# A planner that counts VectorE's and GpSimd's shared port, keeps margins in VectorE's order, and clears the output later

## The chip, the cores and the metric

One core of one Trainium2 chip. The metric is the device time of the whole program in microseconds, the median of three runs. Engines are called PE (TensorE, products), DVE (VectorE), ACT (ScalarE), POOL (GpSimd) and SP (SyncE, which here issues the DMAs).

## What is computed

Three layers in a row: attention with random features, a dense layer of experts ("moe") and a layer that sends each token to one of eight experts ("moe2"). Inputs to `moe` are float64 in memory.

```python
def phi(x):                                   # q, k: 2 x 8 x 576 x 64, omega: 128 x 64
    proj = np.einsum('bhsd,md->bhsm', x, omega)
    h = proj - np.sum(x * x, axis=-1, keepdims=True) / 2.0
    return np.exp(h - np.max(h, axis=-1, keepdims=True)) / np.sqrt(m)
kv = np.einsum('bhsm,bhsd->bhmd', k_p, v); z = np.sum(k_p, axis=2)
x = num / den                                 # 1152 tokens x 512
...
h = x @ w_in                                  # 512 x 2048
g = h * np.clip(h + 3.0, 0.0, 6.0) / 6.0
x = g @ w_out                                 # 2048 x 512
...
expert_idx = np.argmax(x @ w_gate, axis=1)    # 8 experts, at most 288 tokens each
h = np.maximum(np.einsum('ecd,edf->ecf', disp, w1), 0.0)
y = np.einsum('ecf,efd->ecd', h, w2)
out[i] = gate_w[i] * y[expert_idx[i], pos[i]] # rows of tokens left out stay 0
```

## The kernel before

**Products in two halves.** Each float32 operand of the large products is kept as two float32r tiles, a high part (a copy on ScalarE) and a low part (operand minus high part, on VectorE or GpSimd), and a product is three matmuls.

**Attention** runs over 18 units (4 heads' worth of rows each, k and q mixed). A unit has a high part `XH` (ScalarE, L778), a low part `XL` (L780; units 2 to 17 on GpSimd), two halves of feature products `B` (PE, L790, into one of two `pj` buffers, for five units partly `tp`), the row maximum `N` of each half (VectorE, L796, `nm`), four exponentials `P` (ScalarE, L802, `phi`), for k the sums `K` (L817), for q a transposition `C`/`T` (L847, L851), the product with the sums `D` (L863, `nd`), the division `R`, `S`, `X` (VectorE, L873 to L885), a transposition `E` (L891) and the two halves of the token tile, `EH` (ScalarE) and `EL` (VectorE, L917).

**The first expert layer.** w_in and w_out are 16 blocks each, called i0 to i15 and o0 to o15, in groups of four (i0 to i3, o0 to o3, i4 to i7, ...). A block is loaded as int64 words into one of four `raw` buffers and unpacked by five passes `W0` to `W4` (L248, L250, L252, L254, L256) on VectorE; `W4` frees the `raw` buffer for the next load. For blocks from the thirteenth on (o4 and later), the first pass is an absolute value on ScalarE (L246). A block of w_in is then halved: `w` (ScalarE, L262) and `WL`, the low part (L264; before on GpSimd for i0 to i7, on VectorE for i8 to i15). The hidden product `H` of block f for token group g (three groups of 384 tokens) is 12 matmuls on PE (L277, tile `hp`, alternately in two `pj` and four `tp` buffers of PSUM), followed by `Ht` (ScalarE, L281), the gate product `Hg` (VectorE, L285, tile `g`) and a store `Hs` on SP (L287, for group 0 a second, L290). Of w_out each block is transposed on PE, `T` (L299, tile `tpW`, after its `W4`), copied by ScalarE (L302), and folded with the gate's weights once four are there (`G`, L309; `U`, L318), for the gate's logits `L` (L334). Three or four products `H` already stand between the last units of attention.

**After that** come the routing (small operations on VectorE), the products with w_out for 288 chosen tokens (L571), the expert's two layers (L639, L661, L689) for two windows, and indirect writes of the rows to `out`, which has been cleared before (`clear_out`: GpSimd blanks a tile, SP writes it to all of `out` by one DMA of 2304 KB).

**What sets the order.** `Plan` is a list scheduler that runs while the program is built. Each step has an engine, a cost in us, steps it comes after, buffers that it takes and frees, and a rank. `order` repeatedly takes, over all engines, the step that can begin first, and on one engine the lowest rank among those that can begin at once. The begin is the latest of: the engine's free time, `early`, and the end of what it comes after plus a hop. The steps are emitted in that order, so each engine's queue is the planner's; on the chip an engine works its queue in order and waits for data by semaphores alone. No time of the plan is enforced. For attention's steps `DELTA` adds a number to the rank by kind of step and by third of the units (0: units 0 to 4, 1: 5 to 12, 2: 13 to 17); the numbers come from a search over plans. SP's loads stand in the order of `LOADS`, each after a buffer has come free.

## Time and profile before

| what | value |
|---|---|
| runs shown | 331.89 us median (331.43 to 333.74) |
| the profiled execution | 332.73 us, its span 330.9 us |
| PE busy | 306.9 us (93%) |
| VectorE busy | 222.3 us (67%) |
| ScalarE busy | 177.5 us (54%) |
| GpSimd busy | 65.4 us (20%) |
| mean granted clock of TensorE | 0.990 |

How to read the rows below. A row of the windows has, for a stretch in us from the span's start, its length, the busy us of PE, PE's weight loads, VectorE, ScalarE and GpSimd, each with its number of instructions in brackets, then the granted clock (1.00 is full speed), the share of time that the DMA engines were busy, and GB/s. A row of the waits says which engine and line waited for which, then us in total, times, and the longest. A row in order of time has the start, us, the engine, line, operation, tiles, shapes and number, and in square brackets idle time just before it and what ended that. A row of the groups has the number of instructions, busy us and the mean in ns, and then idle time before them. The chain's rows have start, us and what. A row of the DMA issues has the number, KB each and the median us from issue to landing. `hp` is the hidden product, `tpW` the transposed w_out, `nm` the row maximum, `phi` the exponential, `x` and `wo` are blocks of w_in and w_out being unpacked.

### The profile page before, as it was taken

What the parts mean: (1) busy time and instruction counts of PE and PEld (TensorE: products, weight loads), DVE (VectorE), ACT (ScalarE), POOL (GpSimd) and SP (SyncE); (2) the same over time, 40 slices, a digit from 0 to 9 for tenths busy, and PEclk for the clock granted to TensorE, in tenths of its full rate; (3) what the DMA queues carried; (4) which work ended last, traced back from release to release, by engine and by line L of the source; (5) the groups of instructions that cost most, each with busy time, mean ns of one, the idle gap of its engine ahead of it and who ended that gap; (6) DMA issues with size and microseconds to landing.
All of it is one profiled execution on the core that took longest, in us unless ns stands there. A gap on an engine that the chain in (4) does not pass through costs nothing.

```text
span 330.9 us, 6974 instructions
## 1 busy us (share of the span) xinstructions
PE 306.9 (93%) x2570; PEld 278.7 (84%) x2570; DVE 222.3 (67%) x474; ACT 177.5 (54%) x427; POOL 65.4 (20%) x68
## 2 busy tenths in 40 slices
PE   8985989999997798999999999898999999999992
PEld 5884978999987596887989888698999989999781
DVE  5589899999999889889985354749955002764100
ACT  6988799984643545453766324533555132633110
POOL 0774813400240000000000000411513012511021
PEclk9998999999999999999999999999999999999998
DMA  7998662124458777877235127891770004710011
GB/s 245 362 317 309 248 231 66 64 90 137 138 176 254 263 226 234 271 229 223 97 127 184 49 74 244 280 318 57 235 255 1 2 24 101 274 50 0 4 48 32
DMA packets 29675, 54.10 MB, mean 163 GB/s; under 512 B 5536, under 2 KB 18208, under 8 KB 29632
## 3 DMA queue, kind: packets, MB, share of 16 engines
q1 hardware_dynamic: 29248, 52.38, 48.2%
q0 software_dynamic: 384, 1.18, 1.1%
q8 instruction: 22, 0.36, 0.5%
q14 instruction: 21, 0.17, 0.2%
HBM read 37.42 MB, written 16.13 MB: 162 GB/s over the span
## 4 chain that ended last, share of the span: by engine, by line
PE 51%; DVE 15%; DMA 15%; issue 9%; ACT 4%; POOL 2%; SPq 1%; POOLq 0%; ACTq 0%; DVEq 0%
PE hp L277 14%; PE yw L571 14%; PE hp L639 6%; DMA raw<-in_w_in_dram 4%; PE yq L661 4%; PE pj L790 4%; DMA raw<-in_w_out_dram 3%; PE nd L863 3%; DVE nm L796 2%; DMA rawe<-in_w_dram 2%; PE lg L334 2%; DMA out_dram<-scratch,to 2%; DVE g L285 2%; DMA rawx<-in_k_dram 2%; DVE x L252 2%
## 5 line engine op out<-in xcount | busy, mean ns | idle before, releaser
L277 PE MATMUL hp<-xT,wsplit 128*128 128x384 f32 x576 | 107.8, 340 | 0.0
L277 PEld LDWEIGHTS hp<-xT,wsplit 128*128 128x128 f32 x576 | 98.9, 188 | 5.1 <-issue 5.0
L618 POOL TENSOR_TENSOR wsplit<-rawe,wsplit 128x512 fp32r<-128x512 f32 x16 | 22.0, 1379 | 160.6 <-ACT wsplit L616 141.6
L571 PE MATMUL yw<-gh,ohi 128*128 128x288 f32 x256 | 51.9, 298 | 0.2 <-ACT scratch L701 0.2
L281 ACT ACTIVATE t<-hp,three 128x384 f32<-128x384 f32 x48 | 27.6, 578 | 31.4 <-PE hp L277 30.1
L802 ACT ACTIVATE phi<-pj,nm 128x128 f32<-128x128 f32 x144 | 41.0, 414 | 5.5 <-DVE nm L796 5.4
L571 PEld LDWEIGHTS yw<-gh,ohi 128*128 128x128 f32 x256 | 40.8, 188 | 1.3 <-issue 0.6
L285 DVE SCALAR_TENSOR_TENSOR g<-t,hp 128x384 f32<-128x384 f32 x48 | 26.4, 549 | 18.3 <-ACT t L281 17.5
L564 DVE TENSOR_TENSOR gh<-gw,gh 128x288 fp32r<-128x288 f32 x32 | 18.0, 578 | 30.1 <-ACT gh L562 27.8
L571 PE MATMUL yw<-gh,olo 128*128 128x288 f32 x128 | 37.6, 294 | 0.0
L790 PE MATMUL pj<-wbd,xh 128*128 128x256 f32 x144 | 26.3, 305 | 6.5 <-ACT phi L802 5.7
L796 DVE TENSOR_REDUCE nm<-pj 128x4 f32<-128x512 f32 x36 | 24.6, 684 | 5.5 <-ACT phi L802 3.6
L790 PEld LDWEIGHTS pj<-wbd,xh 128*128 128x128 f32 x144 | 19.7, 192 | 10.1 <-ACT phi L802 7.6
L780 POOL TENSOR_TENSOR xl<-rawx,xh 128x512 fp32r<-128x512 f32 x16 | 21.7, 1361 | 30.7 <-ACT xh L778 17.5
L562 ACT ACTIVATE gh<-gw 128x288 fp32r<-128x288 f32 x32 | 14.0, 442 | 23.7 <-PE yw L571 21.1
L639 PE MATMUL hp<-dT,wsplit 128*128 128x288 f32 x192 | 26.3, 296 | 0.4 <-DVE dT L583 0.4
L639 PEld LDWEIGHTS hp<-dT,wsplit 128*128 128x128 f32 x192 | 25.7, 188 | 0.6 <-DVE dT L583 0.6
L571 PEld LDWEIGHTS yw<-gh,olo 128*128 128x128 f32 x128 | 24.1, 189 | 0.0
L616 ACT ACTIVATE wsplit<-rawe 128x512 fp32r<-128x512 f32 x32 | 19.0, 622 | 1.3 <-DMA rawe<-in_w_dram 1.1
L264 POOL TENSOR_TENSOR wsplit<-x,wsplit 128x512 fp32r<-128x512 f32 x8 | 11.6, 1450 | 29.9 <-ACT wsplit L262 29.9
L689 PE MATMUL yp<-wsplit,h 128*96 128x512 f32 (+1 forms) x96 | 16.9, 337 | 0.0
L689 PEld LDWEIGHTS yp<-wsplit,h 128*96 128x96 f32 x96 | 13.5, 162 | 3.4
(147 smaller groups left out, 454.0 us busy)
## 6 DMA issues: line engine op xcount, KB each, us to landing
gall<-g SPq DMA_DIRECT2D x48, 192.0 KB, 3.1
raw<-in_w_in_dram SPq DMA_DIRECT2D x16, 512.0 KB, 4.8
raw<-in_w_out_dram SPq DMA_DIRECT2D x16, 512.0 KB, 4.7
rawe<-in_w_dram SPq DMA_DIRECT2D x16, 512.0 KB, 5.3
gfirst<-g SPq DMA_DIRECT2D x16, 192.0 KB, 3.7
rawx<-in_q_dram SPq DMA_DIRECT2D x9, 256.0 KB, 6.4
out_dram<-blank SPq DMA_DIRECT2D x1, 2304.0 KB, 9.3
gw<-gfirst SPq DMA_DIRECT2D x16, 144.0 KB, 2.6
```

Of the source, the lines that this page charges most:

```text
L277: nc.tensor.matmul(hp, lhsT=w[:, a, wk], rhs=xT[g][b_][:, kk, :], start=(n == 0), stop=(n == 3 * KD - 1))
L281: nc.scalar.activation(out=t, in_=hp, func=ACTF.Relu, bias=three[:, 0:1])
L285: nc.vector.scalar_tensor_tensor(out=gv, in0=t, scalar=6.0, in1=hp, op0=ALU.min, op1=ALU.mult)
L571: nc.tensor.matmul(self.ps[kk], lhsT=wohalf[f][a][:, kk * 128:(kk + 1) * 128], rhs=self.gh[f][:, b_, :], start=(f == YORDER[0] and n == 0) ...
L616: nc.scalar.activation(out=hi, in_=part, func=ACTF.Copy)
L618: engine.tensor_tensor(out=lo, in0=part, in1=hi.bitcast(F32), op=ALU.subtract)
L639: nc.tensor.matmul(hp, lhsT=self.w[0, f][:, a, kk * 128:(kk + 1) * 128], rhs=self.window.dT[b_][:, kk, :], start=(n == 0), stop=(n == 3 * ...
L689: nc.tensor.matmul(ps_, lhsT=self.h2[f // 4, a][:, f % 4, c * SR:(c + 1) * SR], rhs=self.w[1, f][:, b_, x * w:(x + 1) * w], start=(n == 0) ...
L780: (nc.gpsimd if u in X_POOL else nc.vector).tensor_tensor(out=lo[:, sl], in0=rawt[u][:, sl], in1=hi[:, sl].bitcast(F32), op=ALU.subtract)
L790: nc.tensor.matmul(pj[:, 2 * jj:2 * jj + 2, :], lhsT=a[:, j, :], rhs=w, start=(jj == 0 and n == 0), stop=(n == 2), skip_group_check=True,)
L796: nc.vector.tensor_reduce(out=nm, in_=pj, axis=AX.X, op=ALU.max, negate=True)
L802: nc.scalar.activation(out=phis[u][:, 4 * half + h, :], in_=pj[:, h, :], func=ACTF.Exp, bias=nm[:, h:h + 1])
```

## The change

The planner now has a port as well as engines. Steps on VectorE and GpSimd whose names match a pattern (VectorE: `W0` to `W4`, `WL`, `XL`, `OL`, `ol`, `gl`, `v`; GpSimd: `XL`, `WL`, `v`) can only begin, in the plan, when the last such step on either engine has ended. A step can have a `lag`, which the plan adds to the time at which its inputs are there: 1.0 us for the gate products `Hg` of blocks 0 to 9, 1.5 us for the transpositions `T` of w_out. Loads on SP cost more in the plan. The low part `WL` is on GpSimd for i0 to i3 alone, and the first pass `W0` is on ScalarE from i4 on. The clearing of `out` may begin at 58 us of the plan, with a rank ahead of other SP steps. The numbers in `DELTA` are new (one pair stands in the diff). Work on the engines is otherwise the same.

```diff
-    def add(self, name, engine, cost, emit, after=(), takes=None, frees=(), rank=0.0, early=0.0, then=()):
+    def add(self, name, engine, cost, emit, after=(), takes=None, frees=(), rank=0.0, early=0.0, lag=0.0, then=()):
...
+            port=bool(re.match(r"(XL|WL|v)\d*" if engine == "Pool" else r"(W[0-9L]|XL|OL|ol|gl|v\d)", name)) and engine in ("DVE", "Pool"),
-            rank=rank + self.shift, early=early, end=None, then=list(then), kind=self.kind(name),
+            rank=rank + self.shift, early=early, lag=lag, end=None, then=list(then), kind=self.kind(name),
...
+        port = [0.0]
...
-            return max(free_at[st["engine"]], st["early"], t + self.into.get(st["engine"], 0.0) if t else 0.0)
+            return max(port[0] if st["port"] else 0.0, free_at[st["engine"]], st["early"], t + self.into.get(st["engine"], 0.0) + st["lag"] if t else 0.0)
...
+            if st["port"]:
+                port[0] = st["end"]
...
-    ABS_FROM = 12
+    ABS_FROM = 8
+    POOL_TO = 4
+    LAG_G, LAG_T = 1.0, 1.5
+    OUT_AT = 58.0
...
-    DELTA = {'consts': 172.4, ...
+    DELTA = {'consts': 179.8, ...
...
+    on_pool = set(wlist[:POOL_TO])
...
-        (nc.vector if key in abs_act else nc.gpsimd).tensor_tensor(out=t[:, 1, :], in0=xf, in1=t[:, 0, :].bitcast(F32), op=ALU.subtract)
+        (nc.gpsimd if key in on_pool else nc.vector).tensor_tensor(out=t[:, 1, :], in0=xf, in1=t[:, 0, :].bitcast(F32), op=ALU.subtract)
...
-        load(f"w{i}", lambda: w_fetch(wlist[i]), 1.46, "raww")
+        load(f"w{i}", lambda: w_fetch(wlist[i]), 1.65, "raww")
...
-    load("out", clear_out, 6.6)
-    plan.named["Lout"]["after"].append("consts")
+    plan.add("Lout", "SP", 0.5, clear_out, after=["consts"], rank=-960.0, early=OUT_AT)
...
-            (f"Hg{me}", "DVE", 0.47, dict(after=[f"Ht{me}"], takes="g", frees=[f"H{me}", f"Ht{me}"], rank=-500 + n)),
+            (f"Hg{me}", "DVE", 0.47, dict(lag=LAG_G if f < F1T - TAIL else 0.0, after=[f"Ht{me}"], takes="g", frees=[f"H{me}", f"Ht{me}"], rank=-500 + n)),
...
-                (f"T{f}o", "PE", 0.44, dict(after=[f"W4o{f}"] + attended, takes="tp", frees=[f"W0o{f}"], rank=NG * (f - BLOCK) + 0.6)),
+                (f"T{f}o", "PE", 0.44, dict(lag=LAG_T, after=[f"W4o{f}"] + attended, takes="tp", frees=[f"W0o{f}"], rank=NG * (f - BLOCK) + 0.6)),
```

The lines of the changed kernel are ten higher in most of the body (L277 is L287, L299 is L309, L256 is L266, L796 is L806).

What this moves, first on PE, where the transposition of o4 stands in the first expert layer. Before (`wo_1652` is o4; `wsplit_717` and `wsplit_1072` are i2 and i3; xT00 and xT10, xT01 and xT11, xT02 and xT12 are the tokens of groups 0, 1 and 2):

```order
L277 MATMUL hp_1734<-xT02_98,wsplit_717 128x384
L299 MATMUL tpW_1759<-ident_81,wo_1652 128x128 x4
L277 MATMUL hp_1767<-xT00_94,wsplit_1072 128x384
L277 MATMUL hp_1767<-xT10_95,wsplit_1072 128x384
L277 MATMUL hp_1767<-xT00_94,wsplit_1072 128x384 x2
```

And in the changed kernel (`wo_1691` is o4, `wsplit_1635` is i4):

```order
L287 MATMUL hp_1810<-xT10_95,wsplit_1635 128x384
L287 MATMUL hp_1810<-xT00_94,wsplit_1635 128x384
L309 MATMUL tpW_1833<-ident_81,wo_1691 128x128 x4
L287 MATMUL hp_1841<-xT01_96,wsplit_1635 128x384
L287 MATMUL hp_1841<-xT11_97,wsplit_1635 128x384
```

The transposition stood behind the last product of i2; it now stands behind the first product of i4, with the three of i3 and that one between. The same holds for o5 to o12: each stands four products later (o11 three).

Second on VectorE, from the last row maximum of attention on. Before (`wo_1329` is o3, whose first pass lies ahead of this piece; x, rd and nd are the divisions of two units):

```order
L796 TENSOR_REDUCE nm_1365<-pj_1335 128x4
L250 TENSOR_SCALAR wo_1329<-wo_1329 128x512
L873 TENSOR_SCALAR rd_1378<-nd_1345 128x4
L873 TENSOR_SCALAR rd_1393<-nd_1346 128x4
L875 RECIPROCAL rd_1378<-rd_1378 128x4
L885 TENSOR_TENSOR x_1377<-nd_1345,rd_1378 128x256
L875 RECIPROCAL rd_1393<-rd_1393 128x4
L885 TENSOR_TENSOR x_1377<-nd_1346,rd_1393 128x256
L252 TENSOR_SCALAR wo_1329<-wo_1329 128x512
L254 SCALAR_TENSOR_TENSOR wo_1329<-raw_861,wo_1329 128x512
L256 SCALAR_TENSOR_TENSOR wo_1329<-raw_861,wo_1329 128x512
```

And in the changed kernel (`wo_1201` is o0, `wo_1382` is o1):

```order
L806 TENSOR_REDUCE nm_1356<-pj_1338 128x4
L885 RECIPROCAL rd_1346<-rd_1346 128x4
L885 RECIPROCAL rd_1354<-rd_1354 128x4
L895 TENSOR_TENSOR x_1345<-nd_1303,rd_1346 128x256
L895 TENSOR_TENSOR x_1345<-nd_1304,rd_1354 128x256
L266 SCALAR_TENSOR_TENSOR wo_1201<-raw_632,wo_1201 128x512
L258 TENSOR_SCALAR wo_1382<-raw_832 128x512
L260 TENSOR_SCALAR wo_1382<-wo_1382 128x512
L262 TENSOR_SCALAR wo_1382<-wo_1382 128x512
L264 SCALAR_TENSOR_TENSOR wo_1382<-raw_832,wo_1382 128x512
L927 TENSOR_TENSOR xT11_97<-tpE_1392,xT01_96 128x4x64
```

Behind the last row maximum four passes of o3 were left to do of the first two groups of blocks; now the last pass of o0 and all of o1, o2 and o3 are. Counted over the whole queue, 36 passes stood ahead of that row maximum, and 24 do now.

Third on SP, around the clearing of `out`. Before:

```order
L222 DMA raw<-in_w_out_dram 128x512 x2
L380 DMA out_dram<-blank 128x9x512
L728 DMA rawx<-in_q_dram 128x512 x2
L222 DMA raw<-in_w_out_dram 128x512 x2
L220 DMA raw<-in_w_in_dram 128x512 x3
```

And in the changed kernel:

```order
L738 DMA rawx<-in_q_dram 128x512 x3
L230 DMA raw<-in_w_out_dram 128x512 x2
L390 DMA out_dram<-blank 128x9x512
L230 DMA raw<-in_w_out_dram 128x512
L297 DMA gall_101<-g 128x384
L300 DMA gfirst_117<-g 128x384
L228 DMA raw<-in_w_in_dram 128x512
```

The DMA from `blank` stood ahead of the last two loads of q and of o2 and o3; it now stands behind all loads of q and that of o2, ahead of the load of o3 and the first stores.

## Rows read from the trace of the kernel before

**Rows 1.** Busy time by stretch (the windows).

```profile
10.00:20.00 10.00, 9.36 (x141) 8.68 (x142) 6.75 (x11) 10.00 (x36) 8.63 (x19) 1.00 0.96 347
20.00:35.00 15.00, 10.84 (x95) 9.47 (x95) 13.11 (x22) 11.92 (x39) 8.46 (x8) 0.89 0.78 269
35.00:53.00 18.00, 16.81 (x246) 15.16 (x246) 17.65 (x37) 15.79 (x49) 8.13 (x6) 1.00 0.71 249
53.00:72.00 19.00, 18.75 (x242) 17.84 (x242) 18.56 (x49) 18.91 (x60) 5.13 (x4) 1.00 0.09 30
80.00:100.00 20.00, 19.36 (x148) 17.32 (x147) 19.33 (x33) 10.65 (x21) 5.66 (x4) 1.00 0.49 155
100.00:150.00 50.00, 44.05 (x317) 39.03 (x320) 43.83 (x85) 26.86 (x51) 0.00 (x0) 1.00 0.79 247
150.00:212.00 62.00, 60.93 (x396) 53.02 (x390) 41.86 (x97) 30.53 (x60) 3.71 (x3) 1.00 0.46 153
```

**Rows 2.** Waits, whole span.

```profile
ACT phi L802 <- DVE nm L796: 5.4, 9, 1.1
PE tpW L299 <- DVE wo L256: 5.3, 4, 2.0
```

**Rows 3.** PE in order of time, three instructions that waited.

```profile
30.53 0.83 PE L790 MATMUL pj<-wbd,xh 128*128 128x256 f32 x4 [1.88 <-ACT phi L802]
...
101.06 0.66 PE L299 MATMUL tpW<-ident,wo 128*128 128x128 f32 x4 [1.70 <-DVE wo L256]
...
149.43 0.33 PE L318 MATMUL wogt<-ident,wogT 128*128 128x128 f32 x1 [1.24 <-ACT wogT L315]
```

**Rows 4.** Windows: the stretch at the lower clock.

```profile
32.00:34.00 2.00, 2.00 (x33) 1.88 (x32) 1.57 (x4) 1.70 (x6) 2.00 (x2) 0.50 0.14 57
```

**Rows 5.** VectorE's groups of instructions by line and shape.

```profile
L285 DVE SCALAR_TENSOR_TENSOR g<-t,hp 128x384 f32<-128x384 f32 x48 | 26.4, 549 | 18.3 <-ACT t L281 17.5 <-DMA raw<-in_w_out_dram 0.2
...
L256 DVE SCALAR_TENSOR_TENSOR x<-raw,x 128x512 int32<-128x512 int32 x16 | 14.3, 896 | 0.4
...
L252 DVE TENSOR_SCALAR x<-x 128x512 int32<-128x512 int32 x16 | 9.6, 603 | 0.3
L252 DVE TENSOR_SCALAR wo<-wo 128x512 int32<-128x512 int32 x16 | 8.3, 522 | 0.3
...
L264 DVE TENSOR_TENSOR wsplit<-x,wsplit 128x512 fp32r<-128x512 f32 x8 | 5.5, 687 | 0.1
L248 DVE TENSOR_SCALAR x<-raw 128x512 int32<-128x512 int32 x8 | 4.0, 496 | 0.8 <-DMA raw<-in_w_in_dram 0.8
```

**Rows 6.** VectorE in order of time, behind attention.

```profile
87.52 1.68 DVE L256 SCALAR_TENSOR_TENSOR x<-raw,x 128x512 int32<-128x512 int32 x1
...
93.14 0.42 DVE L248 TENSOR_SCALAR x<-raw 128x512 int32<-128x512 int32 x1
...
98.06 1.49 DVE L252 TENSOR_SCALAR wo<-wo 128x512 int32<-128x512 int32 x1
...
100.31 0.69 DVE L256 SCALAR_TENSOR_TENSOR wo<-raw,wo 128x512 int32<-128x512 int32 x1
...
101.72 0.42 DVE L252 TENSOR_SCALAR wo<-wo 128x512 int32<-128x512 int32 x1
```

**Rows 7.** GpSimd in order of time.

```profile
16.41 0.53 POOL L358 TENSOR_TENSOR summed<-ident 128x8 f32<-128x8 f32 x3
...
20.11 0.10 POOL L375 MEMSET carry<- 128x8 bf16 x1
...
97.97 1.30 POOL L264 TENSOR_TENSOR wsplit<-x,wsplit 128x512 fp32r<-128x512 f32 x1 [2.48 <-ACT wsplit L262]
```

**Rows 8.** The chain that ended last: three hidden products in a row.

```profile
158.55 6.26 PE hp L277 x36
```

**Rows 9.** Waits of SP's own queue.

```profile
SPq L380 <- POOL blank L379: 6.2, 1, 6.2
```

**Rows 10.** DMA issues by line.

```profile
out_dram<-blank SPq DMA_DIRECT2D x1, 2304.0 KB, 9.3
```

More of the change, by code (lines that the diff above doesn't have):

```diff
@@ L163, in moe_kernel @@
     IN_TP = {(u, 1) for u in range(5)}
-    X_POOL = set(range(2, 18))
+    X_POOL = set(range(2,18))
     LOADS = "x0 x1 v00 x2 x3 v01 x4 vR x5 x6 x7 x8 x9 v10 w0 x10 x11 v11 w1 x12 x13 x14 g x15 x16 x17 w2 w3 w4 w5 w6 w7 w8 w9 w10 w11"
@@ L172, in moe_kernel @@
     SPLITS = ["PDPDPDPDPDPDPDPD", "PDPDPDPDPDPDPDPD"]
-    ABS_FROM = 12
+    ABS_FROM = 8
+    POOL_TO = 4
+    LAG_G, LAG_T = 1.0, 1.5
+    OUT_AT = 58.0
     SLACK = dict(DVE=0.14)
-    DELTA = {'consts': 172.4, 'XH0': 7.9, 'XL0': 162.8, 'OM': 17.4, 'OL': -135.3, 'B0': -35.7, 'N0': -102.4, 'P0': 43.4, 'XH1': 5.0, 'XL1': -25.3, 'B1': -28.8, 'N1': -83.0, 'P1': 52.0, 'XH2': 412.1, 'XL2': -95.8, 'B2': -8.2, 'N2': 67.1, 'P2': -3.7, 'KT': 274.4, 'K0': -8.3, 'KW': 141.3, 'KV': -15.6, 'K1': 15.7, 'C1': 127.6, 'T1': 91.1, 'D1': 17.2, 'R1': 27.8, 'S1': -0.4, 'X1': 178.6, 'E1': 182.5, 'EH1': 45.1, 'EL1': -150.5, 'C2': -8.8, 'T2': 158.1, 'D2': 96.9, 'R2': 12.6, 'S2': 129.1, 'X2': 17.9, 'E2': -20.4, 'EH2': 146.6, 'EL2': -87.9, 'KR': -30.3}
+    DELTA = {'consts': 179.8, 'XH0': 114.8, 'XL0': 28.0, 'OM': 177.0, 'OL': -70.0, 'B0': 22.8, 'N0': 31.9, 'P0': -12.3, 'XH1': -17.1, 'XL1': -201.3, 'B1': -72.7, 'N1': -23.2, 'P1': 171.6, 'XH2': 385.8, 'XL2': -65.0, 'B2': 92.4, 'N2': -38.4, 'P2': 35.8, 'KT': -7.5, 'K0': -121.6, 'KW': 261.7, 'KV': -47.8, 'K1': 249.5, 'C1': 139.8, 'T1': -17.3, 'D1': -25.2, 'R1': 118.8, 'S1': 7.3, 'X1': 130.4, 'E1': 174.3, 'EH1': -25.3, 'EL1': -122.5, 'C2': -83.5, 'T2': -52.0, 'D2': 233.9, 'R2': -10.8, 'S2': 38.3, 'X2': 208.0, 'E2': -40.8, 'EH2': 72.5, 'EL2': -34.9, 'KR': 36.9}
     RANK = {'A': 0.91, 'B': 1.33, 'C': -3.05, 'D': 2.59, 'E': 3.57, 'EH': 1.06, 'EL': 0.01, 'K': 3.55, 'KV': 3.01, 'N': -2.07, 'P': 2.42, 'R': -1.78, 'T': 3.38, 'XH': -3.59, 'XL': -0.61}
@@ L945, in load_x @@
         for n in range(len(parts)):
-            load(f"x{u}" + "z" * n, lambda: next(gen, None), 0.73 if len(parts) == 1 else 0.47, None if n else "rawx")
+            load(f"x{u}" + "z" * n, lambda: next(gen, None), 0.83 if len(parts) == 1 else 0.47, None if n else "rawx")
     def load_vs(b, c):
-        load(f"v{b}{c}", lambda: load_v(b, c), 1.48, "rawv")
+        load(f"v{b}{c}", lambda: load_v(b, c), 1.7, "rawv")
     load("om", load_omega, 0.47)
@@ L955, in moe_kernel @@
         elif x == "vR":
-            load(x, load_vrest, 1.48)
+            load(x, load_vrest, 1.7)
         elif x[0] == "v":
@@ L1115, in moe_kernel @@
                 (f"w{nm}", "ACT", 0.56, dict(after=[f"W4{nm}"], takes="wa", rank=-300)),
-                (f"WL{nm}", *(("DVE", 0.6) if (kd, f) in abs_act else ("Pool", 1.25)), dict(after=[f"w{nm}"], frees=[f"W0{nm}"], rank=n if (kd, f) in abs_act else -300)),
+                (f"WL{nm}", *(("Pool", 1.25) if (kd, f) in on_pool else ("DVE", 0.6)), dict(after=[f"w{nm}"], frees=[f"W0{nm}"], rank=-300 if (kd, f) in on_pool else n)),
             ]
```

## The prediction

> **What bounds the kernel now.** I read the busy time by stretch first [rows 1]. In each row compare a stretch's length with what each engine was busy. From 20 to 35 us TensorE (PE) lacks 4.16 us of 15 while VectorE (DVE) is busy 13.11; from 35 to 53 PE lacks 1.19 of 18 and VectorE is busy 17.65. So in the first part of attention VectorE is the full engine. From 53 to 72 PE (18.75 of 19) and ScalarE (18.91) are both full, so nothing that only lightens VectorE can shorten that stretch. From 80 to 150, the first expert layer, PE lacks 0.64 + 5.95 = 6.59 us and VectorE has 19.33 of 20, then 43.83 of 50. From 150 on PE is full again (60.93 of 62): what is saved earlier moves everything behind it forward, and I carry it to the end in full.
>
> Then I asked what the idle engines waited for [rows 2]. PE waited 5.3 us in four waits of the transpositions of w_out (`tpW`) for the last unpacking pass of the same block (L256). The first of them cost 1.70 us at 101.06; a fifth wait of 1.24 us, at 149.43, is for a copy on ScalarE [rows 3]. Together 6.5: that is the whole gap of that layer. In attention ScalarE waited 5.4 us in nine waits for row maxima (`nm`), and PE behind it for ScalarE; after the wait of 1.88 us before 30.53 [rows 3] the granted clock stood at 0.50, the lower of the two levels (1.2 GHz of 2.4), through 32 to 34 us [rows 4].
>
> **Why VectorE is full.** The same pass on the same shape takes very different times [rows 5]. Undisturbed, L252 takes 0.42 us, L256 0.69 and L248 0.42 [rows 6]; the means of L252 on x and wo are 0.603 and 0.522, of L256 on x 0.896, of L248 on x 0.496. The excess is 16 x 0.18 + 16 x 0.10 + 16 x 0.21 + 8 x 0.08 = 8.5 us. Four cases lie in the expert layer, the first at 87.52 (1.68 for 0.69) and the last at 98.06 (1.49 for 0.42): 1.0 us each, 4.0 in all [rows 6]. The last began 0.09 us after a GpSimd subtraction (97.97 to 99.27) and ended 0.28 us after it [rows 7]: VectorE's pass stood still until GpSimd's was through. So 8.5 - 4.0 = 4.5 us are lost in attention.
>
> The Trainium skill ("SBUF — State Buffer", section "Who interferes with whom") says that VectorE and GpSimd share a pair of ports as an exclusive lock, that the one that issues first keeps it for its whole instruction, and that row maxima (`tensor_reduce`) never contend. The trace agrees: the 0.28 us above. By the same rule a planner's bookkeeping prevents nothing, since the lock goes by the order on the chip; that speaks against this change, and its outcome is the rival "collisions stay" below.
>
> **The change part by part.**
> 1. Four subtractions `WL` (i4 to i7) leave GpSimd for VectorE, and with them the four collisions of the expert layer, since no GpSimd subtraction is left there: -4.0 us of VectorE, + 4 x 0.69 = +2.7 [rows 5]. The first pass of the same four blocks goes to ScalarE: -4 x 0.42 = -1.7 [rows 6]. ScalarE is busy 10.65 of 20 and 26.86 of 50 there [rows 1], so it takes them at no cost; were it full, they would cost their own 4 x 0.6.
> 2. Attention's order. Before the last row maximum VectorE now does 24 unpacking passes where it did 36: block o0's last pass, all of o1 and o2 and o3's first are moved behind it, 0.69 + 2 x 2.64 + 0.42 = 6.4 us, a block being 3 x 0.42 + 2 x 0.69 = 2.64 [rows 6]. Together with up to 4.5 us of collisions VectorE is some 11 us lighter there. What attention gains is bounded by what stands full next: from 20 to 35 ScalarE has 3.08 us to give (15 - 11.92), from 35 to 53 PE has 1.19 [rows 1]; 4.3 in all, plus 1.0 if the stretch at half clock (2 us at 0.50) goes too. Below, 0. The waits run in a ring (product, row maximum, exponential, product buffer), so a quicker VectorE shortens one link of it and not the others: I take half, **2.1 us**.
> 3. The transpositions of w_out. `LAG_T` and the port move each by four products on PE (one by three): the first (o4) stood behind i2's third product and now stands behind i4's first. Four products take 4 x 2.09 = 8.4 us (three take 6.26) [rows 8]. The pass that it waits for comes later too: +6.4 of moved passes, +2.7 - 1.7 - 4.0 of item 1, and three more gate products ahead of it (3 x 0.55 [rows 5]), together +5.0. PE arrives 8.4 later and the pass ends 5.0 later, against a wait of 1.70 today: 1.7 us to spare. The four waits go: **5.3 us** gained; bounds 0 (they stay) and 6.59 (the fifth goes as well). `LAG_G` only lets VectorE put a pass ahead of a gate product; behind that product hang the next use of its PSUM buffer and its store, and six PSUM buffers (two plus four) cover several products of 2.09 us. At nothing; if the cover were gone, one pass of 0.69.
> 4. Clearing `out`. Today it stands on SP's queue before two loads of q and waits 6.2 us there for GpSimd's blank tile [rows 9]; its transfer takes 9.3 us [rows 10] amid stretches with the DMA engines 0.71 to 0.78 busy. Now it stands behind the load of o2 and is due when the share is 0.09 [rows 1]. Behind it stand the load of o3 and the first stores; o3 is unpacked after the last row maximum, so up to 9.3 us of delay is covered. At nothing; bounds -1 and +1.
> 5. GpSimd's constants (16.41 to 20.21, 3.8 us [rows 7]) now stand before the low part of unit 6 instead of unit 7. ScalarE is busy 10.00 of 10 there with exponentials of earlier units [rows 1], which hides it; uncovered it costs up to 3.8. The changed load costs are only the planner's.
>
> **Sum.** The profiled run took 332.73 us: the span of 330.9 and 1.83 around it. 332.73 - 5.3 - 2.1 = 325.3. The median of the runs shown, 331.89, lies 0.84 below the profiled run, so I forecast **324.5 us**, -2.2%. All upper bounds together (6.59 + 4.3 + 1.0) give 320.8 and, less 0.84, 320.0.
>
> **The rivals**, each from 332.73 and less 0.84.
> - *Collisions stay.* Nothing on the chip holds GpSimd back when its subtraction is ready, so the passes in attention still meet them and attention gains nothing; the expert layer's gain holds, as GpSimd is idle there. For it: the old plan too expected other times than the chip gave. Against: 12 passes fewer are there to meet. 332.73 - 5.3 - 0.84 = 326.6.
> - *The waits stay.* VectorE is 19.33 of 20 full behind attention, and 6.4 us of passes land there. If it runs more than the 1.7 us to spare later than I count, o4 to o7 wait again; all four as today leaves attention's gain alone: 332.73 - 2.1 - 0.84 = 329.8, no change.
> - *Attention gets worse (slower).* The new order makes PE wait for exponentials throughout, as it does today only from 20 to 35 (4.16 of 15, 28%): from 20 to 72 that is 14.4 us against 4.16 + 1.19 + 0.25 = 5.6 today, so +8.8. 332.73 + 8.8 - 5.3 - 0.84 = 335.4. It decides once PE's idle time in attention passes 5.6 + 5.3 = 10.9 us. For it: that stretch is packed to 18.75 of 19 now, and a searched order can only lose there. Against: its passes are fewer.
>
> **How the numbers follow.** The forecast has a chance of 0.55, "collisions stay" 0.20, "the waits stay" 0.15, "attention gets worse" 0.10. The forecast's own range is 320.0 to 327.5. The range that should hold the time 8 times in 10 goes from 320.0 to 330.8: it takes in the first two rivals with 1 us on top, and leaves out most of the third rival. About 1% is what a measurement of this kernel can tell from no change, 328.6 to 335.2 here. Faster by over 1%: the forecast and "collisions stay", 0.75. Within: "the waits stay" and a little of the last, 0.17. Slower: 0.08.
>
> **What would show it.** In the profile after: no wait of `tpW` for w_out's last pass above 0.5 us, and PE idle under 2 us in the 70 us behind attention (step 3); L264 gone from GpSimd there and no pass of 1.4 us on VectorE behind attention (step 1); means of L252 and L256 in attention within 0.1 us of 0.42 and 0.69 ("collisions stay" if not); ScalarE's wait for row maxima down from 5.4 to about 3 (step 2); the blank transfer at 55 to 70 us with nothing waiting for it (step 4). I am wrong if attention's last products end no earlier than today, or if PE waits for low parts of w_in, which it does not do today.

## The result

The changed kernel takes **322.43 us** (median of 4 runs, 321.8 to 322.81) against 331.85 us of the kernel before beside it (4 runs): a ratio of 0.970, interval 0.966 to 0.974. The forecast was 324.5 us, with a range from 320.0 to 330.8. Ratios leave out the executions that ran in the chip's slower state, so a ratio can differ a little from the quotient of the two medians beside it. Its profiled run took 322.81 us with a span of 321.1; the kernel before had 332.73 and 330.9.

Where the time went is read from three marks. Each is the start of the last (or first) instruction of a kind on PE: attention's last transpositions (`tpE`), the last weighting products of the first expert layer (`wogp`), the first products of the second (`yw`). In the rows of a tile, "x to y" are the first and the last start in us. The kernel before:

```profile
L891 PE MATMUL tpE<-ident,x x36: 270/272/275, 40.8 to 81.8; 128*128 128x128 f32 x36
L309 PE MATMUL wogp<-woT,wg x128: 272/273/297, 88.0 to 179.4; 128*32 128x128 f32 x128
L571 PE MATMUL yw<-gh,ohi x256: 290/294/402, 212.3 to 294.5; 128*128 128x288 f32 x128
```

The changed kernel (its lines stand ten further down):

```profile
L901 PE MATMUL tpE<-ident,x x36: 270/273/276, 34.4 to 79.7; 128*128 128x128 f32 x36
L319 PE MATMUL wogp<-woT,wg x128: 272/273/297, 92.2 to 170.3; 128*32 128x128 f32 x128
L581 PE MATMUL yw<-gh,ohi x256: 288/294/402, 202.6 to 284.3; 128*128 128x288 f32 x128
```

Attention ends 2.1 us earlier (81.8 to 79.7). From there to the last weighting product it is 90.6 us instead of 97.6: **7.0 us**. Up to the second layer it is 32.3 instead of 32.9, and from its first product to the end 118.5 instead of 118.6. The sum is 9.8 us, the difference of the spans, where the forecast had 2.1 + 5.3 = 7.4. Of the 7.0, 6.2 are idle time of PE that went (6.59 to 0.40); PE runs the same instructions between the two marks, and what made the rest 0.8 us shorter is not known.

The windows of the changed kernel (from:to, length, then busy time of PE, weight loads, VectorE, ScalarE and GpSimd, then granted clock, DMA share and GB/s), to be laid beside [rows 1]:

```profile
10.00:20.00 10.00, 8.48 (x112) 7.54 (x110) 4.52 (x7) 8.55 (x28) 8.34 (x20) 1.00 0.88 319
20.00:35.00 15.00, 13.32 (x166) 11.95 (x163) 10.62 (x22) 13.92 (x46) 6.61 (x6) 1.00 0.74 253
35.00:53.00 18.00, 16.92 (x245) 15.06 (x243) 16.82 (x37) 16.67 (x52) 6.71 (x6) 1.00 0.21 66
53.00:72.00 19.00, 18.93 (x242) 17.98 (x242) 18.27 (x50) 18.25 (x57) 6.79 (x6) 1.00 0.57 196
80.00:100.00 20.00, 20.00 (x151) 18.14 (x150) 19.26 (x38) 12.10 (x24) 0.00 (x0) 1.00 0.72 234
100.00:150.00 50.00, 49.60 (x357) 44.88 (x356) 45.90 (x89) 28.41 (x54) 0.00 (x0) 1.00 0.84 261
150.00:212.00 62.00, 61.52 (x412) 54.30 (x411) 42.06 (x101) 32.47 (x65) 4.89 (x4) 1.00 0.55 182
```

PE lacks 0.40 us from 80 to 150 (6.59 before). From 20 to 35 it gains 2.48 us and the granted clock is 1.00 instead of 0.89; from 10 to 20 it loses 0.88. VectorE is 58.0 us busy from 10 to 80, where it was 63.8.

The waits of the changed kernel (total, times, longest), beside [rows 2]: no `tpW` on `wo` is among them any more, and ScalarE's wait for row maxima has fallen from 5.4 to 2.1.

```profile
PE pj L800 <- ACT phi L812: 3.2, 7, 0.7
ACT phi L812 <- DVE nm L806: 2.1, 5, 0.9
```

The spare time of the transpositions, on VectorE and on PE: the last pass of o4 ends at 102.64, its transposition starts at 105.49, 2.85 us later.

```profile
101.95 0.69 DVE L266 SCALAR_TENSOR_TENSOR wo<-raw,wo 128x512 int32<-128x512 int32 x1
...
105.49 0.60 PE L309 MATMUL tpW<-ident,wo 128*128 128x128 f32 x4
```

### The profile page after: what moved, and what is told of

The parts are those of the page before. It is cut to its first block, busy times and chain, and to the rows that moved or that the text cites. A ratio compares the mean times of both kernels' runs of the same rounds, so it can differ in the third digit from the quotient of the medians.

```text
span 321.1 us, 6967 instructions
## 1 busy us (share of the span) xinstructions
PE 306.1 (95%) x2570; PEld 279.3 (87%) x2570; DVE 214.4 (67%) x474; ACT 179.8 (56%) x431; POOL 57.1 (18%) x64
## 4 chain that ended last, share of the span: by engine, by line
PE 59%; DVE 11%; DMA 10%; issue 9%; ACT 7%; POOL 1%; SPq 1%; POOLq 0%; DVEq 0%; ACTq 0%
PE hp L287 21%; PE yw L581 14%; PE hp L649 7%; DMA raw<-in_w_in_dram 5%; PE pj L800 5%; PE yq L671 4%; ACT phi L812 3%; PE lg L344 2%; DMA out_dram<-scratch,to 2%; DMA rawx<-in_k_dram 1%; DVE g L295 1%; PE tpC L857 1%; DVE nm L806 1%; PE nd L873 1%; PE tpW L309 1%
## 5 line engine op out<-in xcount | busy, mean ns | idle before, releaser
L287 PE MATMUL hp<-xT,wsplit 128*128 128x384 f32 x576 | 108.3, 341 | 0.1
L287 PEld LDWEIGHTS hp<-xT,wsplit 128*128 128x128 f32 x576 | 98.9, 188 | 5.7 <-issue 4.1
L812 ACT ACTIVATE phi<-pj,nm 128x128 f32<-128x128 f32 x144 | 41.7, 436 | 3.2 <-DVE nm L806 2.1
L574 DVE TENSOR_TENSOR gh<-gw,gh 128x288 fp32r<-128x288 f32 x32 | 15.8, 508 | 28.8 <-ACT gh L572 27.5
L806 DVE TENSOR_REDUCE nm<-pj 128x4 f32<-128x512 f32 x36 | 24.7, 688 | 12.4 <-PE pj L800 10.0
L790 POOL TENSOR_TENSOR xl<-rawx,xh 128x512 fp32r<-128x512 f32 x16 | 20.6, 1299 | 29.4 <-ACT xh L788 29.4
L661 DVE SCALAR_TENSOR_TENSOR h<-hp,h 128x288 fp32r<-128x288 f32 x16 | 7.3, 458 | 13.6 <-ACT h L659 13.6
```

Of the source, the lines that this page charges most:

```text
L287: nc.tensor.matmul(hp, lhsT=w[:, a, wk], rhs=xT[g][b_][:, kk, :], start=(n == 0), stop=(n == 3 * KD - 1))
L790: (nc.gpsimd if u in X_POOL else nc.vector).tensor_tensor(out=lo[:, sl], in0=rawt[u][:, sl], in1=hi[:, sl].bitcast(F32), op=ALU.subtract)
L806: nc.vector.tensor_reduce(out=nm, in_=pj, axis=AX.X, op=ALU.max, negate=True)
L812: nc.scalar.activation(out=phis[u][:, 4 * half + h, :], in_=pj[:, h, :], func=ACTF.Exp, bias=nm[:, h:h + 1])
```

## The experiments

The change mixes six edits. The port, the lags, the split of the work and the place of the clearing were put into the kernel before alone, or taken out of the changed kernel alone, or both; the new margins and the planner's load costs were not. The table has all kernels; the numbers in the first five columns come from one trace each, as above. "Lengthened" counts unpacking passes (L248 to L256, ten lines further down behind the change) from 10 to 81 us that took over 0.15 us more than 0.42 or 0.69, with their excess in us, summed from the rows in order of time. "Gate wait" is what VectorE stood idle from 80 to 150 us in front of gate products (`g`) whose `t` ScalarE had not finished. The ratio is to the kernel before on the same chip.

| kernel | attention's end | from there to last `wogp` | PE idle 80–150 | lengthened | gate wait | ratio, interval |
|---|---|---|---|---|---|---|
| before | 81.8 | 97.6 | 6.59 | 12, 7.0 | 4.7 | 1 |
| changed | 79.7 | 90.6 | 0.40 | 6, 5.3 | 0.8 | 0.970 (0.966–0.974) |
| b_lag: lags alone | 82.0 | 93.6 | 2.56 | 13, 8.3 | 0.7 | 0.989 (0.986–0.993) |
| b_lagG: gate lag alone | 82.9 | 94.7 | 3.35 | 12, 7.1 | 0 | 0.998 (0.994–1.001) |
| b_split: new split alone | 84.5 | 95.5 | 4.58 | 13, 8.3 | 4.6 | 0.996 (0.991–1.001) |
| b_port: port alone | 83.9 | 95.2 | 2.28 | 5, 5.1 | 5.7 | 0.988 (0.979–0.997) |
| a_no_port: changed, no port | 85.2 | 90.8 | 0.83 | 12, 8.4 | 0 | 0.989 (0.982–0.995) |
| a_no_lag: changed, no lags | 80.4 | 93.1 | 1.78 | 6, 5.3 | 4.0 | 0.978 (0.970–0.985) |
| a_no_lagT: changed, gate lag only | 80.8 | 91.2 | 0.84 | 6, 6.0 | 0.5 | 0.975 (0.969–0.980) |
| a_pool_same_order: changed, i4 to i7 subtracted on GpSimd | 79.4 | 90.7 | 0.55 | 6, 6.1 | 1.1 | 0.967 (0.961–0.973) |
| a_out_early: changed, old place of the clearing | 79.6 | 89.8 | 0.00 | 5, 4.4 | 1.2 | 0.971 (0.967–0.976) |
| after_again: changed, second time | 79.5 | 90.6 | 0.41 | 6, 6.0 | 1.4 | 0.970 (0.966–0.974) |
| x_pool4: changed, two low parts on VectorE | 78.2 | 90.2 | 0.00 | 5, 4.2 | 1.2 | 0.968 (0.964–0.973) |
| x_pool4_again: the same, second time | 78.9 | 92.6 | 1.83 | 5, 4.2 | 1.5 | 0.967 (0.963–0.971) |

The column of attention's end has the clock in it as well. The granted clock was 0.57 from 31 to 35 us in the traces of the kernel before and of b_lagG, 0.57 from 8 to 12 and again from 28 to 32 in b_split, 0.53 from 25 to 36 in b_port, and 1.00 from 0 to 80 in all others. So the ends in these four traces cannot be laid to the order alone.

### The four collisions of the expert layer

```diff
-        (nc.gpsimd if key in on_pool else nc.vector).tensor_tensor(out=t[:, 1, :], ...
+        (nc.gpsimd if key in on_pool or key in wlist[8:12] else nc.vector).tensor_tensor(out=t[:, 1, :], ...
```

> The changed kernel, order of all engines unchanged, but the four subtractions of i4 to i7 are carried out by GpSimd again, where VectorE's order has them. Four passes of 0.69 us leave VectorE, and if each of the four subtractions meets a pass as in the kernel before (1.0 us each) VectorE is 4.0 - 2.8 = 1.2 us later. Theory A (the spare time takes it): under 2.85 us, no wait, 322 to 323.5. Theory B (the collisions were what made PE wait): PE waits for w_out's last passes or for low parts of w_in again, 2 us or more, 324.5 or more.

Measured: 322.74 us (0.967), the changed kernel's time. All four collisions are back, VectorE in order of time (first and last):

```profile
89.96 1.66 DVE L264 SCALAR_TENSOR_TENSOR x<-raw,x 128x512 int32<-128x512 int32 x1
...
101.16 1.41 DVE L264 SCALAR_TENSOR_TENSOR wo<-raw,wo 128x512 int32<-128x512 int32 x1
```

The transposition of o4 now has less room, the last pass on VectorE and the transposition on PE:

```profile
102.61 0.69 DVE L266 SCALAR_TENSOR_TENSOR wo<-raw,wo 128x512 int32<-128x512 int32 x1
...
105.11 0.60 PE L309 MATMUL tpW<-ident,wo 128*128 128x128 f32 x4
```

It ends at 103.30 and PE comes at 105.11: 1.81 us are left of 2.85. The four cost 0.7 to 1.1 us each. So the price of a collision was read about rightly, and in this order it costs PE no time. Theory B of this run falls.

### The lags

In the kernel before, with a `lag` added to a step's earliest time in the planner:

```diff
-            return max(free_at[...], st["early"], t + self.into.get(...) if t else 0.0)
+            return max(free_at[...], st["early"], t + self.into.get(...) + st["lag"] if t else 0.0)
-            (f"Hg{me}", "DVE", 0.47, dict(after=...
+            (f"Hg{me}", "DVE", 0.47, dict(lag=1.0 if f < F1T - TAIL else 0.0, after=...
-                (f"T{f}o", "PE", 0.44, dict(after=...
+                (f"T{f}o", "PE", 0.44, dict(lag=1.5, after=...
```

> The kernel before with the two lags alone. The transpositions of o4 to o7 keep their places on PE (behind i2's third product and after); gate products on VectorE come later against the passes. Theory A (the lags open no room without the split: the four collisions are still there): the waits remain, 4 us or more, and the time is that of the kernel before within 1.5 us. Theory B (it is the lag on the gate products that puts o4's passes earlier, as o4's last pass begins at 101.95 us with the lags and at 104.59 without): the waits fall by 2 us or more and so does the time.

Measured: 329.07 us, 1.1% under the kernel before, 4.0 us less from attention's end to the last `wogp`, with the collisions all still there. Theory A of this run, which was mine, falls. What the lag removes is seen on VectorE from 80 to 150 us. The kernel before, waits of VectorE:

```profile
DVE g L285 <- ACT t L281: 4.7, 7, 1.2
```

and the kernel with the lags:

```profile
DVE g L285 <- ACT t L281: 0.7, 1, 0.7
```

VectorE takes its instructions in order. Where a gate product stands ahead of a pass and ScalarE has not finished its `t`, VectorE stands idle and the pass behind it waits too, although its data are there. The kernel before, VectorE in order of time, and the transposition on PE that waits for the pass:

```profile
107.93 0.69 DVE L254 SCALAR_TENSOR_TENSOR wo<-raw,wo 128x512 int32<-128x512 int32 x1
109.80 0.55 DVE L285 SCALAR_TENSOR_TENSOR g<-t,hp 128x384 f32<-128x384 f32 x1 [1.18 <-ACT t L281]
110.27 0.68 DVE L256 SCALAR_TENSOR_TENSOR wo<-raw,wo 128x512 int32<-128x512 int32 x1
...
111.10 0.63 PE L299 MATMUL tpW<-ident,wo 128*128 128x128 f32 x4 [2.00 <-DVE wo L256]
```

The same block with the lags: the gate product no longer waits, and the last pass begins 3.35 us earlier.

```profile
105.85 0.69 DVE L254 SCALAR_TENSOR_TENSOR wo<-raw,wo 128x512 int32<-128x512 int32 x1
106.45 0.55 DVE L285 SCALAR_TENSOR_TENSOR g<-t,hp 128x384 f32<-128x384 f32 x1
106.92 0.69 DVE L256 SCALAR_TENSOR_TENSOR wo<-raw,wo 128x512 int32<-128x512 int32 x1
```

The column "gate wait" follows this without an exception: 0 to 1.5 us in every kernel that has the gate lag, 4.0 to 5.7 in the four that have not.

Then the lag on gate products alone:

> The kernel before with the lag on gate products alone (1.0), the transpositions without one; o4's transposition stands two to three instructions earlier on PE than with both lags. With both lags the waits for w_out were gone (0.20 us) and the last weighting products came 3.8 us earlier. Theory A (the lag on gate products does it, as it lets VectorE do o4 to o7's passes first): the last products of attention at 81 to 82.5, from them to the last weighting product 94 to 95 us as with both lags (93.5; 97.5 before), waits of w_out under 1.5 us, about 1% below the kernel before. Theory B (the lag on the transpositions is needed): waits of 3 us or more, within 1 us of the kernel before.

Measured: 332.19 us against 332.98 (0.998, up to 1.001): no gain that can be told. VectorE's gate waits are gone, but the planner, which now sees the passes earlier, also puts the transposition of o4 one product earlier on PE. With the gate lag alone, PE:

```profile
100.67 0.66 PE L299 MATMUL tpW<-ident,wo 128*128 128x128 f32 x4 [2.45 <-DVE wo L256]
103.72 0.65 PE L299 MATMUL tpW<-ident,wo 128*128 128x128 f32 x4 [0.30 <-DVE wo L256]
```

With both lags, PE:

```profile
99.77 0.66 PE L299 MATMUL tpW<-ident,wo 128*128 128x128 f32 x4 [0.20 <-DVE wo L256]
```

The difference of 2.25 us is about one hidden product (2.09). So in the old order the second lag adds to the first: one brings the pass forward, the other keeps PE from coming forward with it. The lag on the transpositions alone was not run, so that both are needed is not shown. Neither theory of this run was right as written: the layer is 2.9 us shorter, as A had it, with one long wait left, as B had it, and attention ended 1.1 us later in this trace.

In the changed kernel both lags were set to zero, then the transpositions' alone (1.0 and 0.0):

```diff
-    LAG_G, LAG_T = 1.0, 1.5
+    LAG_G, LAG_T = 0.0, 0.0
```

> The changed kernel with both lags at zero. o4's transposition keeps its place behind i4's first product, o5 to o8's stand half a product to two products earlier. Theory A (the spare time between o4's last pass and its transposition, 2.85 us in the changed kernel, comes from the port's order): the margin shrinks by no more than 2.1 us and no wait comes back, 321.5 to 323.5. Rival (the lags hold the transpositions off): waits of o5 to o8 of 0.5 us and more, 2 us or more in all, 324.5 or more.

> The changed kernel with the transpositions' lag at zero and the gate products' lag of 1.0 kept. o4's transposition stands one product earlier than in the changed kernel, o5's as well. Without either lag o4's last pass began at 104.59 us (101.95 in the changed kernel) and PE waited 2.1 us in four waits. Theory A (the lag on gate products makes the room): o4's last pass begins at 102 us again; one product less (2.1 us) leaves about 0.7 us of the 2.85 us spare, no wait above 0.5 us, 1 us or less above the changed kernel. Theory B (the lag on the transpositions makes it): waits of 2 us and more in all, as without both lags, 2 to 3 us above the changed kernel.

Measured: 326.08 us without lags (ratio 0.978 against 0.970, intervals that overlap) and 324.18 with the gate lag alone. The traces are clearer than the times: from attention's end to the last `wogp` 93.1 and 91.2 us against 90.6, and without lags PE waits again, from 80 to 150 us:

```profile
PE tpW L309 <- DVE wo L266: 1.8, 3, 1.2
```

The last pass of o4 still ended ahead of PE in both, by 0.85 and 0.39 us instead of 2.85. Without lags the waits came back at later blocks (the longest 1.15 us at 134.09), which my "no wait comes back" had missed. With the gate lag alone the longest wait for a pass is 0.2 us, as its theory A had it. The gate lag gives some 1.9 us of the 2.5, the other lag about 0.6.

### The new split alone

```diff
-    ABS_FROM = 12
+    ABS_FROM = 8
```

> The kernel before with one part of the change alone: the last subtraction of i4 to i7 goes from GpSimd to VectorE and the first pass of these blocks to ScalarE. The order keeps o4's transposition behind i2's third product and 37 passes ahead of the last row maximum. Theory A (the split alone ends the waits): VectorE is 4.0 + 1.7 - 2.7 = 3.0 us lighter ahead of o4's last pass, more than the 1.70 us of the first wait, so PE's four waits (5.3 us) shrink to under 1.5 us; attention as before (last products at 81 us); about 4 us less than the kernel before on the same chip. Theory B (it needs the lags as well): the order puts the passes no earlier, three or four waits remain, 4 us or more, and the time is that of the kernel before within 1.5 us.

Measured: 333.16 us against 332.79 (0.996, up to 1.001). The waits at o4 to o7 are gone, as theory A had it. PE from 100 to 150 us shows what came instead:

```profile
127.40 0.66 PE L299 MATMUL tpW<-ident,wo 128*128 128x128 f32 x4 [1.53 <-DVE wo L256]
130.46 0.66 PE L299 MATMUL tpW<-ident,wo 128*128 128x128 f32 x4 [0.31 <-DVE wo L256]
...
149.40 0.33 PE L318 MATMUL wogt<-ident,wogT 128*128 128x128 f32 x1 [2.03 <-ACT wogT L315]
```

The waits moved to the next group of blocks, ahead of which VectorE again stood for a gate product (4.6 us in all, as before). The layer is 2.1 us shorter, and attention ends 2.7 us later, in a trace with two stretches at the lower clock. The traced execution took 334.0 us at a mean granted clock of 0.985; three others of this kernel took 329.9 to 330.9 at 0.997 to 0.998. So neither theory holds for the time: the split removes the first waits, and a gain by itself can't be told from these times.

### The port: attention's part

The port alone in the kernel before (the planner's lines with `port`, as in the diff of the change), and the changed kernel without it:

```diff
-            port=bool(re.match(...)) and engine in ("DVE", "Pool"),
+            port=bool(re.match(...)) and False,
```

> The kernel before with one part of the change alone: the planner treats the port of VectorE and GpSimd as a resource; the old margins, the old split of the work, the old place of the clearing, no lags. In its order 26 unpacking passes stand ahead of the last row maximum (36 before, 24 after), and the first transposition of o4 stands behind i4's first product, as in the changed kernel. Theory A (the order that the port gives is what gained): PE is idle for under 1.5 us from 80 to 150 us, no wait for w_out's last pass above 0.5 us, and the time is 324 to 326 although GpSimd still subtracts eight low parts of weights. Theory B (the four collisions that went with GpSimd's subtractions are what gained): the waits stay, 328 to 331.

> The changed kernel without the port in the planner; new margins, lags, split and clearing stay. Its order has 38 unpacking passes ahead of the last row maximum, and o4's transposition is back behind i2's third product. Theory A (the order that the port gives is what gained): PE waits three or four times for w_out's last pass, 4 to 5 us from 80 to 150, and attention's last products end no earlier than in the kernel before (81.1); 328 to 331. Theory B (the collisions): GpSimd subtracts nothing in the expert layer, VectorE is 3 us lighter there (4.0 + 1.7 - 2.7), which is more than the 1.70 us of the first wait, so the waits are gone: 323 to 326.

Measured: 331.24 us (0.988, a wide interval to 0.997) and 329.59 (0.989). Either way the waits for o4 to o7 are gone. With the port alone PE comes four products later, as in the changed kernel, and waits of 0.54 and 0.80 us are left at o11 and o12; neither theory of this run holds as written, since the waits went and the time did not follow. Without the port o4's transposition is back at its old place, and the waits stay away all the same: the last pass ends at 97.62, 3.28 us before PE comes, and the layer takes 90.8 us. So theory A of the second run, that it takes the port's order, falls; B was right there, though its time was not, for attention ended 3.4 us later than in the kernel before (81.8 by the mark used here, not 81.1). Windows without the port (the granted clock is 1.00 throughout):

```profile
20.00:35.00 15.00, 12.49 (x160) 11.16 (x156) 14.76 (x27) 13.33 (x44) 6.70 (x6) 1.00 0.83 292
35.00:53.00 18.00, 16.58 (x224) 14.48 (x224) 17.77 (x37) 16.94 (x53) 9.76 (x8) 1.00 0.29 90
53.00:72.00 19.00, 16.95 (x217) 15.26 (x212) 18.48 (x43) 16.65 (x52) 4.32 (x4) 1.00 0.59 197
```

VectorE is full again (14.76 of 15, 17.77 of 18), and PE lacks 2.05 us from 53 to 72 where it lacked 0.25 [rows 1] and 0.07 with the port. The order has 38 passes ahead of the last row maximum and 12 of them are lengthened; with the port it has 24, of which 6 are.

The port with the old margins has 26 passes there and 5 lengthened, VectorE 57.5 us busy from 10 to 80, as light as in the changed kernel; and yet attention ends 2.1 us later than before. Windows with the port alone:

```profile
20.00:35.00 15.00, 11.37 (x84) 10.21 (x83) 11.56 (x16) 10.68 (x34) 6.19 (x6) 0.68 0.67 239
...
28.00:30.00 2.00, 1.94 (x9) 1.94 (x10) 1.22 (x3) 1.81 (x7) 0.32 (x1) 0.50 0.32 83
```

and PE in order of time, the wait ahead of the stretch at 0.50:

```profile
25.14 1.12 PE L793 MATMUL pj<-wbd,xh 128*128 128x256 f32 x4 [2.36 <-ACT phi L805]
```

PE waited 2.36 us for an exponential, and from 26 to 34 us the granted clock stood at 0.50, the level of 1.2 GHz. A VectorE with room to spare (11.56 of 15) did not keep the units from waiting for each other. But what the port alone is worth in attention stays open. The traced execution took 331.58 us at a mean granted clock of 0.978; another one of the same kernel took 328.2 at 0.993. If those 3.4 us lie in attention, it ended there at about 80.5 (an estimate), ahead of the kernel before. What is shown is the other half: with the new margins and without the port attention ends 5.5 us later than with it (85.2 against 79.7), at the full clock in both. The new margins alone with the old planner were not run.

### The clearing of the output

```diff
-    plan.add("Lout", "SP", 0.5, clear_out, after=["consts"], rank=-960.0, early=OUT_AT)
+    load("out", clear_out, 6.6)
+    plan.named["Lout"]["after"].append("consts")
```

> The changed kernel, unedited, once more, as the measure for the two versions beside it on the same chip. Expected: the ratio to the kernel before again at 0.970 within its interval (0.966 to 0.974).

> The changed kernel with the clearing of the output back at its old place among the loads; the order on TensorE, VectorE and ScalarE is the same, only SP and GpSimd differ. If the place is worth nothing, the changed kernel's time within 1 us. If the blank tile holds SP's queue and two loads of q behind it come late (6.2 us of wait in the kernel before), attention's first half slows: units behind those loads late by up to 6 us, and 1 to 4 us above the changed kernel.

Measured: 323.82 and 323.14 us on one chip (0.971 and 0.970), no difference; attention ends at 79.6 and 79.5. The later place moves the traffic (DMA share from 35 to 53 us 0.21 in the changed kernel, 0.60 with the old place), and no engine waited for the transfer, which the changed kernel issues at 58.4 us.

### A version further

The changed kernel loses 0.88 us of PE from 10 to 20 us, where GpSimd makes the low parts of units 2 to 5 one after the other while VectorE is busy 4.52 of 10. Two of them on VectorE instead:

```diff
-    X_POOL = set(range(2,18))
+    X_POOL = set(range(4,18))
```

> A version of the changed kernel: the low parts of units 2 and 3 are subtracted on VectorE instead of GpSimd; nothing else is edited. From 10 to 20 us VectorE is busy 4.52 of 10 in the changed kernel and GpSimd begins unit 2's at 11.33, 1.26 us each. If that chain (low part, product, row maximum, exponential) sets the start, the products of units 2 and 3 come about 0.6 us earlier each and the time is 0.5 to 2 us below the changed kernel; if ScalarE's exponentials set it (8.55 busy of 10), within 0.5 us of it; if the order of the rest suffers, up to 1 us above.

> The version with the low parts of units 2 and 3 on VectorE, unedited, beside the changed kernel on the same chip. Its trace showed attention's last products 1.5 us earlier and PE idle for 2.0 us from 80 to 212 us less than 0.5. If that carries to the end, 1 to 2.5 us less than the changed kernel; if it was the spread between executions, the same within 0.7 us.

Measured: 321.6 us (0.968, interval 0.964 to 0.973), and a second time 322.34 beside 323.14 of the changed kernel (0.967 and 0.970). The mechanism shows in the windows, PE 9.68 and 14.10 where it was 8.48 and 13.32:

```profile
10.00:20.00 10.00, 9.68 (x124) 8.38 (x121) 5.44 (x8) 8.99 (x30) 7.29 (x19) 1.00 0.94 339
20.00:35.00 15.00, 14.10 (x168) 12.77 (x166) 12.04 (x24) 14.63 (x47) 6.41 (x6) 1.00 0.76 259
```

Attention ends 1.5 and 0.6 us earlier than in the changed kernel. In the second trace 1.84 us of it were lost again from 100 to 150 us, for copies on ScalarE that came late (a wait of 1.02 at 145.26), which the first trace does not have. It is the fastest of all by its medians, by 0.8 us; that lies between the two forecasts of the second run and is less than the intervals can tell.

## Why the prediction was right, and where its account was not

- **Attention, forecast 2.1 us.** Measured 2.1. The number was luck, and the account behind it was half right. The 12 passes did leave the stretch, the stretch at half clock went, and ScalarE's wait for row maxima fell to 2.1 (about 3 forecast). But I had all 4.5 us of collisions vanish there. The excess was larger than I counted, 7.0 us, because the passes of L250 and L254, and w_out's of L248 and L256, collide too and I had left them out; and 5.3 us of it remain, in six passes. In the changed kernel, VectorE and the GpSimd subtractions beside the second and the third of these:

```profile
20.98 0.84 DVE L258 TENSOR_SCALAR x<-raw 128x512 int32<-128x512 int32 x1 [0.66 <-DMA raw<-in_w_in_dram]
27.53 1.67 DVE L266 SCALAR_TENSOR_TENSOR x<-raw,x 128x512 int32<-128x512 int32 x1
35.31 1.48 DVE L260 TENSOR_SCALAR x<-x 128x512 f32<-128x512 f32 x1
48.47 1.78 DVE L264 SCALAR_TENSOR_TENSOR x<-raw,x 128x512 int32<-128x512 int32 x1
57.35 1.27 DVE L262 TENSOR_SCALAR x<-x 128x512 int32<-128x512 int32 x1
60.97 1.58 DVE L264 SCALAR_TENSOR_TENSOR x<-raw,x 128x512 int32<-128x512 int32 x1
...
27.37 1.28 POOL L790 TENSOR_TENSOR xl<-rawx,xh 128x512 fp32r<-128x512 f32 x1 [2.85 <-ACT xh L788]
35.23 1.28 POOL L790 TENSOR_TENSOR xl<-rawx,xh 128x512 fp32r<-128x512 f32 x1 [1.08 <-ACT xh L788]
```

  From 10 us to the end of the last row maximum (73.24 before, 71.67 now) VectorE was busy 49.9 us instead of 57.3: 7.4 lighter, not 11. "Half of the bound" hit the number, while with a VectorE as light from 10 to 80 us (the port alone) attention ended later in its trace: the term was a choice that came out, not a calculation. The clock is a rival that nothing here rules out: the kernel before ran from 31 to 35 us at 0.57 and the changed kernel at 1.00, and my 2.1 us had no term for it; how much of the gain it is was not taken apart. The sign I named, means within 0.1 us of 0.42 and 0.69, failed (on w_in's blocks they are 0.63 and 0.93 in attention); of the rival "collisions stay" the mechanism came true in half and its price, no gain in attention, did not.
- **The rule on the port.** The Trainium skill ("SBUF — State Buffer", section "Who interferes with whom") has the shared ports go to the one that starts first, for its whole instruction. The rows agree: the GpSimd subtraction began at 27.37, the pass at 27.53, and the pass ended 0.55 us after the subtraction. I drew from it that a planner's bookkeeping prevents nothing. That was too strong: with the port in the planner 5 or 6 passes are lengthened, without it 12 or 13, in every kernel of the table; part of that is that fewer passes stand in that stretch.
- **The first expert layer, forecast 5.3 us.** Measured 7.0: this is the term that was mis-sized, by 1.7 us, and it came out 0.4 above its bound of 6.59. The four waits went (5.3), PE's idle time from 80 to 150 fell by 6.2 in all, since the fifth wait shrank from 1.24 to 0.40 as well, which I had only in the bound. The sign "PE idle under 2 us" held (0.40).
- **Why the waits went.** My step said: four products later on PE against passes 5.0 us later, 1.7 us to spare. The spare time is 2.85, and relative to attention's end the last pass came 3.7 us later, not 5.0. That PE comes four products later is one way to end the waits and not the only one: without the port PE comes for o4 at its old place, and no wait for it is left. The parts were weighed wrongly. I put the lag on gate products "at nothing"; with its companion it takes 4.0 us off the layer in the old order, and without both the changed kernel loses 2.5 of its 7.0, of which some 1.9 are the gate lag's. The other 4.5 come without any lag, and the parts put in alone take 2.1 (split), 2.4 (port) and 4.0 us (lags) off the layer, together more than the 7.0: they remove the same waits in part, and no single one carries the gain. The row that would have told me of the lag stood in the trace of before: VectorE's 4.7 us in front of gate products from 80 to 150 us, part of the 17.5 in [rows 5]. I had put VectorE down as full there (43.83 of 50) and not asked what the rest waited for. The collisions, my largest term of item 1 (4.0 us), are worth nothing to the time in the new order.
- **The rest of item 1.** With the split, the lags and the new margins in place the layer is 89.8 to 90.8 us, whether GpSimd or VectorE subtracts and with or without the port (92.6 in x_pool4's second trace); with the lags alone 93.6, with the split alone 95.5. Whether the first pass of four blocks on ScalarE (-1.7 us of VectorE) or the new margins give that difference was not taken apart.
- **Items 4 and 5.** The clearing is worth nothing, as forecast. From 10 to 20 us PE lost 0.88 us, which I had at nothing with a bound of 3.8; attention's gain is net of it. I had priced the constants; with two low parts on VectorE instead (x_pool4) PE is busy 1.20 us more there, so it was the first low parts on GpSimd. That the constants cost anything is not shown.
- **The other rivals.** "The waits stay" would have needed the passes 2.85 us later; it comes true in part where the lags are taken out (a_no_lag). "Attention gets worse" decided at 10.9 us of idle time from 20 to 72; PE is idle 2.8 us there in the changed kernel and 6.0 without the port. Its direction came true in five traces of kernels with a part of the change (attention ends 0.2 to 3.4 us later in b_lag, b_lagG, b_port, b_split and a_no_port; three of them ran partly at the lower clock), never its price.

## What to carry to other kernels

Ask of an engine that looks nearly full what its remaining idle time waits for: an instruction that stands in order and waits for another engine holds up all ready work behind it. Letting it stand a little later, and its readers on TensorE with it, here took 4.0 of 6.6 us of TensorE's idle time away. Parts of a re-planned order do not add up: alone in the old order two parts gave 1.1 and 1.2%, two gave nothing that can be told, and all together gave 3.0%; so price a new order as a whole, from which passes stand ahead of which. A collision or a wait is worth what it takes beyond the spare time of the one that waits for it, which is read as the distance from the last pass's end to its reader's start. And read the granted clock before two traces are compared: two executions of one kernel, at 0.978 and 0.993, lay 3.4 us apart here, more than attention's whole gain.
